# A planner that counts late inputs and holds engines for one chain

## The chip, the cores and the metric

The kernel runs on one core of a Trainium2 chip. What is measured is the device time of one execution in microseconds. The core has five engines with a list of instructions each, worked through in order: TensorE (PE in the profile, its weight loads PEld), VectorE (DVE), ScalarE (ACT), GpSimd (POOL) and SyncE (SP), which here issues the transfers.

## What is computed

Block-sparse attention and then a feed-forward layer with a rational function, in float32, for 4 batches, 8 heads, 768 positions and 64 values a head. A row of 32 positions (a block) sees its neighbours, the first and the last block, and three sampled ones; the first and the last block see all.

```
scores = scale * q @ k.T          # masked by blocks
attn   = softmax(scores)
x      = (attn @ v) as 3072 x 512
h      = x @ w_in                 # 512 x 2048
g      = (a0 + a1 h + a2 h^2 + a3 h^3) / (1 + |b0||h| + |b1| h^2 + 1e-6)
out    = g @ w_out                # 2048 x 512
```

## The kernel before

**Work.** Float32 values are carried as pairs of 16-bit values (a high and a low half), scaled by a power of two that comes from a maximum. So k, q, x and w_in each need the maximum of their magnitudes (ScalarE, L400 in `bound`), a transpose on TensorE that spreads it over the partitions (`most` in `scales`, L351), a few tiny VectorE instructions (L356 to L368), the high half (any of three engines, L150 or L154) and the low half (VectorE, L394 for q and k). The halves of k and q are then transposed on TensorE into a bank of PSUM named sp (L683 for k of batches 1 to 3, L758 for q) and copied out by ScalarE (L150 into kt, L762 into qa). From qa two transfers make a swapped copy qc (L766, L767). From kt a transfer stores k to DRAM (L697), from where the sampled blocks are loaded later (L876 to L883).

The attention works on blocks: scores into sp (L911), masked maxima on VectorE (L921), exponentials (L939), transposes (L980), values (L1037). Four blocks make a group that is weighted by VectorE (L1071), transposed (L1109) and cut into the high half xh (L150) and the low half xl (L1125). Eight blocks are a chunk of 256 positions, 12 chunks in all. The feed-forward layer takes a chunk in 8 units: 24 matmuls of 256 columns into ph (L1179 to L1181), some ten instructions of ScalarE and VectorE for the rational function (L1186 to L1224), and 12 matmuls of 512 columns into acc (L1235 to L1237). The first chunk has no scale of its batch yet: its own maximum is taken from the transposed x (L400 on ph, L1094) and goes through `scales` as scx before any unit can begin. Early idle time of TensorE is filled with matmuls of an identity whose result is not used (L162).

**Order.** All of it is written down first as a list of `Op`s: an engine, a price in ns, the ops it comes after, a priority (`prio`, in units of the feed-forward layer), and the buffers that it takes and uses (`Slot` of a `Ring`; two banks for sp, two buffers for qa, one for hlq and ldq, two for hl). `issue` then simulates the engines and emits instructions in the order of that simulation; each engine runs them in that order on the chip, waiting where an input is late. An op becomes ready on an engine at `at`, the end of what it comes after plus a latency by pair of engines plus 17 ns. Among the ops that have their buffers, the one with the smallest key is next: the time at which it could start, less 21 ns but not before the engine is free, then its priority. An op whose priority lies over 8 units ahead of the work begun is passed over.

```
t = max([now[e], o.at[e]] + [s.ring.free[0][0] for s in o.takes])
key = (max(t - slack, now[e]) + (0 if e == o.engs[0] else other[e]), o.prio, o.n)
```

So the order on TensorE follows the planned times of inputs, those of transfers among them, and nothing corrects it on the chip.

Of the kernel before, what the change touches and what calls it, by code (L numbers as in the profile page):

```python
# [23 lines left out]
def kernel(  # L24
# [70 lines left out]

    VE, SC, PO, TE, SY = "DVE", "Activation", "Pool", "PE", "SP"
    LAT = {(SC, TE): 410, (VE, TE): 240, (PO, TE): 225, (TE, SC): 200, (TE, VE): 200, (TE, SY): 170, (VE, SC): 130, (VE, PO): 130,
           (SC, VE): 155, (SC, PO): 180, (PO, VE): 80, (PO, SC): 100}
# [6 lines left out]
    class Ring:  # L105


        def __init__(self, bufs):
            self.free = [(0.0, b) for b in bufs]
# [7 lines left out]
    class Op:  # L117


        def __init__(self, eng, price, run, after=(), prio=0.0, takes=(), uses=(), unit=None, behind=None):  # L120
            self.alt = eng if isinstance(eng, dict) else None
            self.engs = list(eng) if self.alt else [eng]
            self.eng, self.price, self.run, self.prio, self.unit = self.engs[0], price, run, prio, unit
            self.after, self.behind = [a for a in after if a is not None], behind
            self.takes, self.uses = list(takes), list(takes) + list(uses)
            for s in self.uses:
                s.left += 1
            self.next, self.at, self.work = [], dict.fromkeys(self.engs, 0.0), 1.0
            plan.append(self)

    plan = []
# [32 lines left out]
    def issue(ahead):  # L164
# [29 lines left out]
        while left:  # L194
            best = None
            for e, l in todo.items():
                for o in l:
                    if o.prio > clock + ahead or not all(s.ring.free for s in o.takes):
                        continue
                    t = max([now[e], o.at[e]] + [s.ring.free[0][0] for s in o.takes])  # L200
                    if e == SY:
                        t = max(t, lanes[0])
                    if e == VE and held[0] <= t < held[1] and o.run.__name__ not in READS_PSUM:
                        t += HELD * (held[1] - t)
                    key = (max(t - slack, now[e]) + (0 if e == o.engs[0] else other[e]), o.prio, o.n)
                    if best is None or key < best[0]:
                        best = key, t, o, e
# [57 lines left out]
            for x in o.next:  # L265
                if x.behind is not o:
                    for y in x.engs:
                        lat = MARGIN if isinstance(price, list) else OWN.get(e, 0) if y == e else LAT.get((e, y), 160) + MARGIN
                        x.at[y] = max(x.at[y], end + lat)
                x.wait -= 1  # L270
                if not x.wait:
                    for y in x.engs:
                        todo[y].append(x)
# [68 lines left out]

    def scales(get, name, after, prio, slot=(), finish=None, keep=None):

# [30 lines left out]

        a = Op(TE, 109, most, after, prio, takes=[s_ps])
        a = Op(VE, 260, largest, [a], prio, takes=slot, uses=[s_ps])
# [178 lines left out]
    def prep(b, when, what):  # L556
# [11 lines left out]
        for w in what:  # L568
# [40 lines left out]
            if w == 2:  # L609
                def largest(mx=mx):  # L610
                    nc.vector.tensor_reduce(out=mx[0][:, 6:7], in_=mx[0][:, 0:n], axis=AX.X, op=ALU.max)

                o = Op(VE, 75, largest, los, when(w, 0, n - 1))
                q_scale[b] = scales(lambda mx=mx: mx[0][:, 6:7], "scqb", [o], when(w, 0, n - 1))
                continue

            def largest(mx=mx, w=w):
# [4 lines left out]
                           keep=lambda s, inv, w=w: kv[b].__setitem__(2 + w, inv),  # L622
                           finish=out_scale if w and b < PLAIN else None)
            (k_scale, v_scale)[w][b] = o
# [13 lines left out]
    def rest(b, w, j, d, o_scale, sc, prio, before):  # L638
# [59 lines left out]

        o = Op(TE, 445, transposes, [o], prio, takes=[s_ps], uses=[s_hl])
        sk = s_kall[t] if first else s_kt[b]  # L700
# [12 lines left out]
    def prep_q(b, t, prio, before):  # L713
# [57 lines left out]
        if own:  # L771
            o = Op(SC, 613, most, [o_ld], prio, uses=[s_ld])
            o, sc = scales(lambda: d["mx"][:, 0:1], "scq", [o], prio, sl_sc)
        else:
            o, sc = q_scale[b]
# [5 lines left out]
        else:  # L781
            d["first"], d["oc"] = qt[b, 0], qt[b, 0]["oc"]
        x = Op(TE, 445, transposes, [l], prio, takes=[s_ps, d["slot"]], uses=[s_hl])
        x = Op(SC, 904, evac, [x], prio, uses=[s_ps, d["slot"]])
        d["oq"] = Op(SY, [(650, 131072)] * 2, swap, [x], prio, uses=[d["slot"]])
# [44 lines left out]
    def attention(b, j, prio):  # L830
# [245 lines left out]
        oinv = row(VE, [(70, guard), (81, invert)], [o for o in G["ops"] if o.eng != TE], p, uses=[G["s_sm"]])  # L1076
        G["ops"] = [Op(VE, 600, weigh, [o for o in G["ops"] if o.eng == TE] + [oinv], p, takes=[G["s_xn"]], uses=G["av"] + [G["s_sm"]])]
        if c:
            turned(G, c, e2, p)
            evacuate(G, c, e2, p, kv[b], 4, v_scale[b])  # L1080
            return
# [20 lines left out]
        for G, e2, p, _ in x_wait:  # L1102
            evacuate(G, c, e2, p, x_own, 1, o)

    def turned(G, c, e2, p):
# [302 lines left out]
```

## Time and profile before

| | us |
|---|---|
| median of 3 runs | 883.95 |
| the runs | 875.47, 883.95, 887.24 |
| the profiled execution | 879.92 |
| its span | 878.2 |
| TensorE busy | 827.3 (94%) |
| VectorE busy | 725.5 (83%) |
| ScalarE busy | 675.9 (77%) |

The span runs from the first to the last instruction in the profile, and the profiled execution's own time is 1.7 us longer. In the rows further below, "[1.81 <-DVE hlq L394]" behind an instruction says that its engine was idle for 1.81 us before it, and that the VectorE instruction of line 394 that writes hlq ended this. In the table of stretches PEclk is the granted clock of TensorE as a share of 2.4 GHz.

### The profile page before, as it was taken

What the parts mean: (1) busy time and instruction counts of PE and PEld (TensorE: products, weight loads), DVE (VectorE), ACT (ScalarE), POOL (GpSimd) and SP (SyncE); (2) the same over time, 40 slices, a digit from 0 to 9 for tenths busy, and PEclk for the clock granted to TensorE, in tenths of its full rate; (3) what the DMA queues carried; (4) which work ended last, traced back from release to release, by engine and by line L of the source; (5) the groups of instructions that cost most, each with busy time, mean ns of one, the idle gap of its engine ahead of it and who ended that gap; (6) DMA issues with size and microseconds to landing.
All of it is one profiled execution on the core that took longest, in us unless ns stands there. A gap on an engine that the chain in (4) does not pass through costs nothing.

```text
span 878.2 us, 28042 instructions
## 1 busy us (share of the span) xinstructions
PE 827.3 (94%) x10338; PEld 642.6 (73%) x10338; DVE 725.5 (83%) x1746; ACT 675.9 (77%) x1450; POOL 112.3 (13%) x117
## 2 busy tenths in 40 slices
PE   8989868779899899999999999999999899999997
PEld 4456756657678687778878787778778788778886
DVE  6778998999998787787878686888888688778886
ACT  5789988987787788897777687897767587767563
POOL 1146426164300000100000000100000000000000
PEclk9999988998999999999999999999999999999999
DMA  8697799868656966888556956889545965740000
GB/s 195 154 215 224 209 206 202 217 205 215 140 152 169 282 156 175 216 241 229 140 147 177 250 164 172 216 222 242 147 137 160 235 159 155 179 108 26 1 26 24
DMA packets 240216, 151.22 MB, mean 172 GB/s; under 512 B 16208, under 2 KB 222928, under 8 KB 240080
## 3 DMA queue, kind: packets, MB, share of 16 engines
q1 hardware_dynamic: 240080, 149.43, 65.7%
q8 instruction: 82, 1.34, 0.7%
q14 instruction: 54, 0.44, 0.2%
HBM read 132.07 MB, written 11.01 MB: 163 GB/s over the span
## 4 chain that ended last, share of the span: by engine, by line
PE 62%; DVE 11%; DMA 9%; SPq 7%; ACT 6%; issue 3%; POOL 1%; ACTq 0%; POOLq 0%; DVEq 0%
PE acc L1235 8%; PE ph L1179 8%; PE acc L1236 8%; PE acc L1237 8%; PE ph L1180 7%; PE ph L1181 7%; PE av L1037 5%; PE sp L911 4%; PE pt L980 4%; DMA ldq<-in_q_dram 2%; DMA wl<-in_moe_w_in_dram 2%; SPq L1007 1%; DMA vg<-in_v_dram 1%; DMA ld<-in_v_dram 1%; DVE pr L921 1%
## 5 line engine op out<-in xcount | busy, mean ns | idle before, releaser
L1179 PE MATMUL ph<-xh,wi 128*128 128x256 f16 x768 | 214.1, 279 | 4.7 <-DVE tt L1196 3.6
L1181 PE MATMUL ph<-xh,wi 128*128 128x256 f16 x768 | 212.5, 277 | 2.2 <-POOL wi L514 2.2
L1180 PE MATMUL ph<-xl,wi 128*128 128x256 f16 x768 | 212.6, 277 | 0.1
L1235 PE MATMUL acc<-wo_h,gh 128*128 128x512 f32 x376 | 160.8, 428 | 0.0
L1237 PE MATMUL acc<-wo_h,gl 128*128 128x512 f32 x376 | 149.4, 397 | 3.3 <-DVE gl L1224 3.3
L1236 PE MATMUL acc<-wo_l,gh 128*128 128x512 f32 x376 | 149.4, 397 | 0.0
L1203 DVE SCALAR_TENSOR_TENSOR ab<-sq,absb,ab 128x512 f32<-128x512 f32 x96 | 73.4, 764 | 53.4 <-ACT ab L1200 53.3
L1186 ACT ACTIVATE sq<-ph,fc 128x512 f32<-128x512 f32 x96 | 65.8, 685 | 65.9 <-PE ph L1181 65.5
L1179 PEld LDWEIGHTS <-wi 128*128 128x128 f16 x768 | 76.3, 99 | 34.5 <-issue 17.4
L921 DVE CUSTOM_DVE_ANT_1 pr<-sp,bias 128x256 f32<-128x256 f32 x224 | 84.8, 418 | 10.1 <-PE sp L911 10.0
L1214 DVE SCALAR_TENSOR_TENSOR gh<-tt,par,rr 128x512 fp32r<-128x512 f32 x96 | 75.7, 789 | 17.0 <-PE acc L1236 12.2
L939 ACT ACTIVATE pr<-pr,st,cqb 128x256 f32<-128x256 f32 x112 | 66.1, 594 | 29.6 <-DVE st L950 29.4
L1237 PEld LDWEIGHTS acc<-wo_h,gl 128*128 128x128 f32 x376 | 71.0, 189 | 22.2 <-DVE gl L1224 5.1
L1181 PEld LDWEIGHTS <-wi 128*128 128x128 f16 x768 | 76.4, 99 | 12.7 <-POOL wi L514 2.5
L1235 PEld LDWEIGHTS acc<-wo_h,gh 128*128 128x128 f32 x376 | 71.4, 190 | 17.5 <-issue 1.9
L1037 PE MATMUL av<-vg,pT 128*32 128x64 f32 x3584 | 74.4, 224 | 9.5 <-DMA vg<-in_v_dram 5.6
L1180 PEld LDWEIGHTS <-wi 128*128 128x128 f16 x768 | 76.5, 100 | 9.3 <-issue 0.9
L1037 PEld LDWEIGHTS av<-vg,pT 128*32 128x32 f32 x3584 | 56.6, 111 | 34.4 <-issue 11.9
L1236 PEld LDWEIGHTS acc<-wo_l,gh 128*128 128x128 f32 x376 | 71.4, 190 | 11.4
L980 PE MATMUL pt<-ident,pr 128*128 128x128 f32 x448 | 74.8, 288 | 3.3 <-ACT pr L939 3.0
L980 PEld LDWEIGHTS pt<-ident,pr 128*128 128x128 f32 x448 | 67.6, 204 | 13.0 <-ACT pr L939 5.3
L150 ACT ACTIVATE pT<-pt 128x512 f32<-128x512 f32 x112 | 66.5, 593 | 12.5 <-PE pt L980 11.8
(185 smaller groups left out, 1661.0 us busy)
## 6 DMA issues: line engine op xcount, KB each, us to landing
vg<-in_v_dram SPq DMA_DIRECT2D x312, 64.0 KB, 3.1
vg<-in_v_dram SPq DMA_DIRECT2D x88, 192.0 KB, 3.8
vg<-in_v_dram SPq DMA_DIRECT2D x24, 512.0 KB, 5.4
kall<-ks SPq DMA_DIRECT2D x52, 192.0 KB, 3.3
kall<-ks SPq DMA_DIRECT2D x156, 64.0 KB, 2.3
ld<-in_k_dram SPq DMA_DIRECT2D x36, 256.0 KB, 3.5
wl<-in_moe_w_in_dram SPq DMA_DIRECT2D x32, 256.0 KB, 4.9
wl<-in_moe_w_out_dram SPq DMA_DIRECT2D x16, 512.0 KB, 4.3
```

The costliest lines, as they stand in the source:

```text
L150: nc.scalar.activation(out=out, in_=in_, func=AF.Copy, scale=by)
L921: nc.vector.tensor_tensor_reduce(out=prs[x][:, g].rearrange("p (s r) -> p s r", r=BLK), in0=h["sp"][:, g].rearrange("p (s r) -> p s r", r= ...
L980: nc.tensor.transpose(pp[:, jj * P:(jj + 1) * P], cols, ident)
L1037: nc.tensor.matmul(av[rows, g], pT[:, 2 * g + kt, rows] if plain else pT[:, 2 * g + kt, pa_, rows], vf[:, g * HG + h4, kt * D:(kt + 1) * D ...
L1179: nc.tensor.matmul(o, wh, xh[:, :, cc], start=(cc == 0), stop=False)
L1180: nc.tensor.matmul(o, wh, xl[:, :, cc], start=False, stop=False)
L1181: nc.tensor.matmul(o, wl, xh[:, :, cc], start=False, stop=(cc == NCC - 1))
L1203: nc.vector.scalar_tensor_tensor(out=d["ab"], in0=d["sq"], scalar=absb[:, 1:2], in1=d["ab"], op0=ALU.mult, op1=ALU.add)
L1214: nc.vector.scalar_tensor_tensor(out=d["gh"], in0=d["tt"], scalar=par[:, 0:1], in1=d["rr"], op0=ALU.add, op1=ALU.mult)
L1235: nc.tensor.matmul(acc[:, t], ghs, wo_h[:, f], start=(new and e == 0), stop=False)
L1236: nc.tensor.matmul(acc[:, t], ghs, wo_l[:, f], start=False, stop=False)
L1237: nc.tensor.matmul(acc[:, t], gls, wo_h[:, f], start=False, stop=(last and e == 1))
```

## The change

An `Op` gets a number `late` (0 unless given) that is added to the time at which its inputs count as ready, and a number `rush` (0 unless set) that is taken off in the key: an op that could start in up to 600 ns is then chosen ahead of one that could start now, and the engine is kept for it. `late` is 1500 ns for the spreading transposes of the scales of k, v and q in batches 1 to 3 and for the transposes of k and q in these batches; the scales of w_in and of the first chunk's x keep 0. `rush` is set on the second group of the first chunk (chunk 0): its weighting, transposes, maximum, scale, and the halves of x of both groups. Besides, the buffer qa is taken by the copy out of PSUM and no longer by the q transposes in front of it.

```
+    LATE = 1500.0
...
-            self.after, self.behind = [a for a in after if a is not None], behind
+            self.after, self.behind, self.rush = [a for a in after if a is not None], behind, 0.0
...
-                    key = (max(t - slack, now[e]) + (0 if e == o.engs[0] else other[e]), o.prio, o.n)
+                    key = (max(t - slack - o.rush, now[e]) + (0 if e == o.engs[0] else other[e]), o.prio, o.n)
...
-                        x.at[y] = max(x.at[y], end + lat)
+                        x.at[y] = max(x.at[y], end + lat + x.late)
...
-    def scales(get, name, after, prio, slot=(), finish=None, keep=None):
+    def scales(get, name, after, prio, slot=(), finish=None, keep=None, late=0.0):
...
-        a = Op(TE, 109, most, after, prio, takes=[s_ps])
+        a = Op(TE, 109, most, after, prio, takes=[s_ps], late=late)
...
-                q_scale[b] = scales(lambda mx=mx: mx[0][:, 6:7], "scqb", [o], when(w, 0, n - 1))
+                q_scale[b] = scales(lambda mx=mx: mx[0][:, 6:7], "scqb", [o], when(w, 0, n - 1), late=LATE)
...
-                           finish=out_scale if w and b < PLAIN else None)
+                           late=LATE if b else 0.0, finish=out_scale if w and b < PLAIN else None)
...
-        o = Op(TE, 445, transposes, [o], prio, takes=[s_ps], uses=[s_hl])
+        o = Op(TE, 445, transposes, [o], prio, takes=[s_ps], uses=[s_hl], late=0.0 if first else LATE)
...
-            o, sc = scales(lambda: d["mx"][:, 0:1], "scq", [o], prio, sl_sc)
+            o, sc = scales(lambda: d["mx"][:, 0:1], "scq", [o], prio, sl_sc, late=LATE if b else 0.0)
...
-        x = Op(TE, 445, transposes, [l], prio, takes=[s_ps, d["slot"]], uses=[s_hl])
-        x = Op(SC, 904, evac, [x], prio, uses=[s_ps, d["slot"]])
+        x = Op(TE, 445, transposes, [l], prio, takes=[s_ps], uses=[s_hl], late=LATE if b else 0.0)
+        x = Op(SC, 904, evac, [x], prio, takes=[d["slot"]], uses=[s_ps])
...
+        first = len(plan) - 1
         if c:
...
+        for o in plan[first:]:
+            o.rush = 600.0
```

## Rows read from the trace of the kernel before

**Rows 1.** The page: busy us of each engine, its share of the span and its instructions.

```profile
PE 827.3 (94%) x10338; PEld 642.6 (73%) x10338; DVE 725.5 (83%) x1746; ACT 675.9 (77%) x1450; POOL 112.3 (13%) x117
```

**Rows 2.** The table by stretches: from and to, length, then busy us of PE, PEld, DVE, ACT and POOL with their instructions, the granted clock, the busy share of the transfer engines, GB/s.

```profile
100.00:120.00 20.00, 14.17 (x292) 11.30 (x292) 20.00 (x48) 18.50 (x46) 6.89 (x7) 0.96 0.84 169
...
300.00:350.00 50.00, 50.00 (x652) 40.77 (x652) 40.43 (x108) 43.08 (x97) 0.98 (x1) 1.00 0.65 175
```

**Rows 3.** Waits of TensorE at the lines that the change touches, asked for from 100 to 200 us (the first two) and from 200 us to the end: who waited for whom, us in total, times, longest.

```profile
PE sp L683 <- ACT kt L150: 1.9, 2, 1.4
PE sp L758 <- DVE cq L749: 1.4, 1, 1.4
...
PE sp L758 <- DVE hlq L394: 5.5, 3, 2.2
...
PE sp L351 <- DVE mx L618: 0.8, 1, 0.8
...
PE sp L683 <- DVE hl L394: 0.6, 1, 0.6
PE sp L683 <- DVE st L921: 0.6, 1, 0.6
```

**Rows 4.** Timelines of GpSimd, VectorE and TensorE around the waits at 487 and 687 us: start and length in us, instruction, and in brackets the idle time before it.

```profile
487.59 0.69 POOL L154 TENSOR_SCALAR hlq<-ldq,scqb 128x512 f16<-128x512 f32 x1 [37.46 <-DMA ldq<-in_q_dram]
...
488.31 0.75 DVE L394 SCALAR_TENSOR_TENSOR hlq<-ldq,scqb,hlq 128x512 f16<-128x512 f32 x1 [4.45 <-POOL hlq L154]
...
489.12 0.62 PE L758 MATMUL sp<-ident,hlq 128*128 128x128 f16 x8 [1.81 <-DVE hlq L394]
...
684.57 0.28 PE L1179 MATMUL ph<-xh,wi 128*128 128x256 f16 x1
...
685.79 0.27 PE L1181 MATMUL ph<-xh,wi 128*128 128x256 f16 x1
...
688.86 1.04 PE L758 MATMUL sp<-ident,hlq 128*128 128x128 f16 x8 [2.22 <-DVE hlq L394]
689.69 0.42 PE L1179 MATMUL ph<-xh,wi 128*128 128x256 f16 x1
```

**Rows 5.** The table by stretches again (columns as in rows 2), close around three waits at L758.

```profile
490.00:494.00 4.00, 4.00 (x58) 2.65 (x51) 4.00 (x11) 3.50 (x7) 0.00 (x0) 0.57 1.10 350
686.00:692.00 6.00, 3.78 (x52) 2.99 (x52) 3.94 (x10) 1.06 (x3) 0.69 (x1) 0.72 1.10 246
...
548.00:552.00 4.00, 4.00 (x76) 3.21 (x77) 3.86 (x9) 3.02 (x5) 0.00 (x0) 1.00 0.65 179
```

**Rows 6.** Timelines of TensorE, ScalarE and VectorE on the chain of the first chunk's scale.

```profile
64.45 0.60 PE L1109 MATMUL ph<-ident,xn 128*128 128x128 f32 x4
...
65.17 1.00 ACT L863 COPY kx<-kall 128x256 f16 x3
66.08 0.58 ACT L400 ACTIVATE scrap<-ph 128x512 f16<-128x512 f32 x1
...
67.52 4.48 PE L162 MATMUL acc<-ident 128*128 128x512 f16 x20
71.84 0.27 PE L1179 MATMUL ph<-xh,wi 128*128 128x256 f16 x1
...
68.61 0.15 DVE L1097 COPY xs<-scx 128x1 f32<-128x1 f32 x1
...
68.85 1.30 ACT L762 ACTIVATE qa<-sp 128x1024 f16<-128x1024 f16 x1
70.02 1.24 ACT L150 ACTIVATE xh<-ph,xs 128x512 f16<-128x512 f32 x2
...
70.72 1.41 DVE L1125 SCALAR_TENSOR_TENSOR xl<-ph,xs,xh 128x512 f16<-128x512 f32 x2 [1.43 <-ACT xh L150]
...
79.80 0.23 PE L911 MATMUL sp<-kall,qa 128*32 128x96 f16 x4
```

**Rows 7.** Timelines of VectorE and TensorE for the last two q tiles. Of the last but one: the transposes (712.23) and the first score (736.69). Of the last: the low half (716.68), the last score of the tile two back (728.10), the transposes (736.15).

```profile
712.23 0.34 PE L758 MATMUL sp<-ident,hlq 128*128 128x128 f16 x3
...
716.68 0.74 DVE L394 SCALAR_TENSOR_TENSOR hlq<-ldq,scqb,hlq 128x512 f16<-128x512 f32 x1
...
728.10 0.28 PE L911 MATMUL sp<-kall,qc 128*32 128x256 f16 x4
...
736.15 0.33 PE L758 MATMUL sp<-ident,hlq 128*128 128x128 f16 x3
...
736.69 0.29 PE L911 MATMUL sp<-kall,qa 128*32 128x256 f16 x4
```

**Rows 8.** Timelines of SP and TensorE at the start of batches 2 and 3: the first load of sampled k and the first scores; then from the page the time of such a load from issue to landing (issues, KB each, median us).

```profile
398.38 1.82 SPq L878 DMA_DIRECT2D kall<-ks  x1
...
601.22 1.49 SPq L878 DMA_DIRECT2D kall<-ks  x1
...
413.36 0.29 PE L911 MATMUL sp<-kall,qa 128*32 128x256 f16 x4
...
615.41 0.29 PE L911 MATMUL sp<-kall,qa 128*32 128x256 f16 x4
...
kall<-ks SPq DMA_DIRECT2D x52, 192.0 KB, 3.3
```

More of the change, by code (lines that the diff above doesn't have):

```diff
@@ L117, with __init__ @@
     class Op:
-        def __init__(self, eng, price, run, after=(), prio=0.0, takes=(), uses=(), unit=None, behind=None):
+        def __init__(self, eng, price, run, after=(), prio=0.0, takes=(), uses=(), unit=None, behind=None, late=0.0):
             self.alt = eng if isinstance(eng, dict) else None
@@ L127, in __init__ @@
                 s.left += 1
-            self.next, self.at, self.work = [], dict.fromkeys(self.engs, 0.0), 1.0
+            self.next, self.at, self.work, self.late = [], dict.fromkeys(self.engs, 0.0), 1.0, late
             plan.append(self)
```

## The prediction, made before the change was run

> **What bounds the kernel now.** I read four views in this order. First the page's engine rows [rows 1]: TensorE is busy 827.3 of 878.2 us, VectorE 725.5, ScalarE 675.9. Then the table by stretches [rows 2], since one average hides two regimes. From 100 to 120 us VectorE is the full engine (20.00 of 20 us) and TensorE is not (14.17); from 300 to 350 us TensorE is the full one (50.00 of 50 us) while VectorE lies at 40.43. The reader should see that idle TensorE time counts in full only in the second regime, which I let begin at 200 us. Third, the waits of TensorE before and after 200 us [rows 3], of which I keep the lines that end in an instruction the change touches: L758 (transposes of q), L683 (transposes of k), L351 (the transpose that spreads a scale). Fourth, timelines of the places named below.
>
> In the second regime TensorE waited 5.5 us in three waits at the q transposes, 0.8 us at a scale and 0.6 + 0.6 us at the k transposes, together 7.5 us; shorter waits at these lines are left out. The longest two show how such a wait arises [rows 4]: GpSimd had waited for the q load, VectorE stood 4.45 us behind GpSimd, and TensorE, which runs its list in order, stood 1.81 us at the transposes, although what follows them needs neither. At 688 us it is the same with 2.22 us; 5.5 - 1.8 - 2.2 leaves 1.5 us for the third. The order had been written for a load that came sooner.
>
> **The change, part by part.**
>
> *The late price (1500 ns on inputs of preparing transposes, batches 1 to 3).* No instruction is added or removed. The planner now believes that those inputs come 1.5 us later, so it puts about 1.5 us of other TensorE work in front. A wait can shrink by its own length or by 1.5 us, whichever is less: 3 × 1.5 + 0.8 + 0.6 + 0.6 = 6.5 us. That is one end; the other is nothing, if the work put in front waits just as long. For the three long ones the nearest row says that work is at hand: right behind the transposes of 688.86 the matmuls of a feed-forward unit start at 689.69 with no wait named [rows 4], though VectorE had only just come out of its own stop, so their inputs were older. I take these three in full, 4.5 us, and the short ones as nothing, since under a microsecond another late result of VectorE can stand in.
>
> What is queued behind: a transpose that comes 1.5 us later moves the ScalarE copy and, for q, two transfers on SP by as much. The q tile transposed at 712.23 was read only at 736.69 [rows 7], so more than 20 us cover this; should that cover be gone, the delay goes straight into the scores. The k side has less cover and is the last rival.
>
> *The clock.* The granted clock is 1.00, the upper level of 2.4 GHz, from 300 to 350 us [rows 2]. From 490 to 494 us it is 0.57, from 686 to 692 us 0.72 [rows 5]: parts of these stretches lie at the half level (1.2 GHz), and both follow or hold one of the two long waits. Behind the third, at 548 us, the stretch stays at 1.00. The falls cost 4 × 0.43 = 1.7 us and 6 × 0.28 = 1.7 us of TensorE work. With 1.5 us taken off, 0.3 and 0.7 us of these waits are left, less than the wait before 548 us that brought no fall; I take both back, 3.4 us. The other end is 0, if the falls come elsewhere instead.
>
> *The same price before 200 us.* There 1.4 us (L758, released by cq) and 1.9 us (L683) are waited [rows 3]. VectorE is the full engine in that part, so I count nothing; the other end is a gain of 3.3 us.
>
> *The hold of 600 ns for the first chunk's scale.* Its chain is in [rows 6]. The last transposes of the chunk end at 64.45 + 0.60 = 65.05 us, but ScalarE took three copies for the scores at 65.17 and comes to the maximum (L400 on ph) only at 66.08: 1.0 us. The scale is ready at 68.61 + 0.15 = 68.76; ScalarE took the copy of a q tile at 68.85 and scales x at 70.02: 1.2 us. Together 2.2 us that holding could save, while TensorE issued 20 filling matmuls from 67.52 on that compute nothing, and the first real one came at 71.84. The work that is moved behind is covered: the q tile copied at 68.85 is read at 79.80. Soon after comes VectorE's regime, so what counts is idle time of VectorE: it stood 1.43 us before the low half of x (70.72). I take 1.4 us. The bounds: 2.2 us gained, or, as a price, VectorE kept idle for up to 0.6 us by each of its nine rushed instructions (the weighting, two maxima, three steps of the scale, the copy, two low halves), 5.4 us lost in a regime that has no VectorE time to spare.
>
> *The q slot, taken by the copy and no longer by the transposes.* It lets transposes run before the tile two back is done with. The clearest case is the last tile [rows 7]: its low half was ready at 717.42, the slot free at 728.38, yet it was transposed at 736.15, 7.8 us after that: TensorE had more urgent work. So I cost this at nothing. Were it used, a score bank of two would be held for up to 728.4 - 717.4 - 1.5 = 9.5 us, and the loss lies between nothing and those 9.5 us; nearest is the row that shows the transposes late for another reason, so nothing.
>
> **Sum.** The profiled execution took 879.92 us (span 878.2 and 1.7 around it). 879.9 - 4.5 - 3.4 - 1.4 = 870.6 us. It lies 4.0 us below the median of the three runs (883.95), so beside that median the forecast is 874.6, rounded to **875 us**, 1.0% less. A measurement of this kernel can tell about 2% from no change, here 17.7 us: the three runs alone are 11.8 us apart.
>
> **The rivals.**
>
> *The waits move on, nothing is gained (884 us, the median).* The cause at 487 and 687 us is a late load and a VectorE that stands 4.45 us behind GpSimd [rows 4]; the price is put on TensorE's instructions and brings neither the load nor VectorE's part sooner. TensorE would then pass the transposes and meet the next late result. For it speaks that VectorE is idle in the same microseconds, against it the unit at 689.69. Chance 0.27.
>
> *TensorE is not truly full (884 us too).* Then it makes up a stop of 2 us by itself, and taking the stop away gives nothing. By the rows it is full: twelve matmuls of 256 columns start from 684.57 to 685.79, 11 steps of 0.111 us [rows 4], beside 256 / 2.4 = 107 ns that the columns alone take at the upper clock, and matmuls stand for 50.00 of 50 us in 300 to 350 us [rows 2]. The Trainium skill, "Perfetto Trace Analysis", section "Identifying the Most-Contended Engine", says that the busy share of matmuls is no measure of how close TensorE is to its limit, and that the busy share of weight loads should be read instead. By that rule the stretch is at 40.77 of 50 us, a fifth would be free, and the stops would cost nothing: 884 us. The spacing speaks against it here: 0.08.
>
> *The k preparation gets too long (slower).* Place: the chain of a batch's k, one scale and six sets of transposes, each priced 1.5 us late. If each link also falls behind a half unit, 12 × 0.111 = 1.3 us [rows 4], a link costs 2.8 us and seven of them 19.6 us. Then the last store of a batch, and the loads of its sampled k behind it on SP, come that much later. Those loads start at 398.38 and 601.22 in batches 2 and 3, land some 3.3 us later, and the first scores follow at 413.36 and 615.41 [rows 8]: slacks of 11.7 and 10.9 us. Where the delay exceeds these it decides; the excess is 7.9 + 8.7 = 16.6 us, so 896.5 us, 900.5 beside the median. With the bare 1.5 us per link (10.5 us) it stays below both, so the chance is 0.10.
>
> **How the numbers follow.** Forecast 0.55, moved waits 0.27, TensorE not full 0.08, long k preparation 0.10. The low end takes every gain at its bound on the profiled execution: 879.9 - 6.5 - 3.4 - 3.3 - 2.2 = 864.5. The high end is the first rival with the holds at their price: 884 + 5.4 = 889.4. At either end I add 3.5 us, as the three runs lie 3.3 to 8.5 us from their own median: 861 to 893. Outside stays most of the k rival and a little on either side. Faster by over 2% (below 866.3) needs nearly all bounds at once: 0.11. Slower by over 2% (above 901.6) is half of the k rival: 0.05. Within 2%: 0.84.
>
> **What would show it.** Right: the waits at L758, L683 and L351 after 200 us fall from 7.5 us to below 4, the stretches near 490 and 690 us show a clock of 1.00, and the first real matmul comes near 70 us, not at 71.84. Moved waits: those lines vanish while the waits for gl, pr or pT grow by as much. Long k preparation: the first scores of a batch wait for the k load. Wrong altogether: a new wait of tens of microseconds in the first 200 us, where the whole order is written anew behind the hold.

## The result, and the profile after

The changed kernel takes 893.57 us (median of 6 runs, 893.22 to 894.45), the kernel before 884.43 us beside it (6 runs, 875.47 to 887.24): a ratio of 1.0144, 95% interval 1.0103 to 1.0185, so 1.4% slower. The forecast was 875 us with 861 to 893, so the time lies 0.6 us above the range. The profiled execution took 893.68 us (span 891.9); before it was 879.92 (878.2).

The page's engine row answers to [rows 1]. TensorE is busy 2.7 us longer in a span 13.7 us longer; the work is the same, it only stands differently.

```profile
PE 830.0 (93%) x10333; PEld 646.5 (72%) x10333; DVE 727.2 (82%) x1748; ACT 673.3 (75%) x1447; POOL 113.2 (13%) x118
```

Where the time went is seen first in the start of the 96 units of the feed-forward layer (the first matmul into ph of each). Unit 0 starts 1.8 us earlier than before. Up to unit 9 the distance jumps (unit 7 starts 13.2 us later, unit 9 1.8 us earlier, at 176.18 against 178.01); unit 10 starts 12.0 us later (205.71 against 193.69), unit 20 15.2 us, and from unit 73 on the distance stays at 14.07 us. So most of the loss is there by 206 us, in the part of the run where I had counted nothing. The table by stretches (columns as in rows 2), first before, then after:

```profile
100.00:150.00 50.00, 38.31 (x602) 30.24 (x603) 45.69 (x120) 44.39 (x106) 18.95 (x18) 0.86 0.92 191
150.00:180.00 30.00, 25.56 (x327) 20.23 (x325) 30.00 (x53) 28.77 (x62) 6.44 (x7) 1.00 0.86 224
180.00:206.00 26.00, 19.88 (x273) 14.75 (x271) 25.61 (x68) 21.49 (x49) 18.52 (x17) 0.87 0.68 192
```

```profile
100.00:150.00 50.00, 42.10 (x691) 32.26 (x689) 46.97 (x118) 46.02 (x115) 18.51 (x18) 0.84 0.91 199
150.00:180.00 30.00, 23.23 (x339) 17.88 (x340) 29.45 (x66) 25.18 (x56) 7.76 (x8) 0.86 0.86 206
180.00:206.00 26.00, 15.38 (x158) 11.46 (x156) 18.62 (x46) 18.92 (x43) 17.47 (x16) 0.74 0.69 220
...
300.00:350.00 50.00, 50.00 (x669) 40.44 (x667) 43.72 (x123) 41.02 (x94) 1.38 (x2) 1.00 0.67 184
```

VectorE, which had 0.4 us of idle time from 150 to 206 us, now stands idle for 7.4 of the last 26 us, and TensorE's clock is 0.74 there. The regime behind it looks as before.

What stopped them between 180 and 206 us, by the longest wait of TensorE from 170 to 215 us and by timelines of TensorE, ScalarE, VectorE and SP:

```profile
PE sp L1113 <- ACT kt L151: 7.6, 1, 7.6
```

```profile
179.71 1.10 PE L684 MATMUL sp<-ident,hl 128*128 128x128 f16 x16
...
183.10 0.65 PE L1038 MATMUL av<-vg,pT 128*32 128x64 f32 x32 [1.17 <-ACT pT L151]
191.39 1.12 PE L1113 MATMUL sp<-ident,xn 128*128 128x128 f32 x4 [7.64 <-ACT kt L151]
192.30 0.42 PE L352 MATMUL sp<-ident,mxq 128*128 128x128 f32 x1
...
185.52 0.79 ACT L1194 ACTIVATE tt<-ph,par,fc 128x512 f32<-128x512 f32 x1
...
188.92 0.63 ACT L151 ACTIVATE wi<-dw 128x512 f16<-128x512 f32 x1 [1.49 <-POOL dw L155]
189.46 2.47 ACT L151 ACTIVATE kt<-sp 128x512 f16<-128x512 f16 x4
...
186.34 0.69 DVE L1197 TENSOR_TENSOR tt<-tt,sq 128x512 f32<-128x512 f32 x1 [3.07 <-ACT tt L1194]
...
192.76 0.29 DVE L357 TENSOR_REDUCE scq<-sp 128x1 f32<-128x128 f32 x1 [2.61 <-PE sp L352]
...
179.68 0.40 SPq L698 DMA_DIRECT2D ks<-kt  x1
```

TensorE transposed the last two k tiles of batch 1 together at 179.71 (sixteen transposes) into the two banks of sp. Their copies go into kt, which is still being stored (issued at 179.68, landed at 185.40), and ScalarE's list reaches them only at 189.46, behind copies of w_in, for one of which it stands idle 1.49 us itself. Until then no bank is free for the x transposes (L1113), and behind these in TensorE's list stands the transpose that spreads the scale of a q tile (L352), for which VectorE waits at 192.76. A second group of stops lies at 157 to 163 us, where TensorE waits 2.90 us for VectorE's masked maxima and 1.58 us for its tt. Its waits from 150 to 170 us:

```profile
PE sp L684 <- DVE st L922: 2.9, 1, 2.9
PE ph L1183 <- DVE tt L1200: 1.9, 2, 1.6
```

To weigh all stops alike I add up **TensorE's lost time** from the timeline: its idle time in front of instructions (the 4.4 to 4.9 us behind its last one are left out), the time of the filling matmuls (L163 after, L162 before), and for real matmuls under a lower clock the part that the clock takes. Before it is 88.9 us up to 206 us and 18.0 us after, together 106.9; in the changed kernel 101.3 and 22.3, together 123.6. What is left of the span is 771.3 and 768.3 us. Of the 12.4 us that are added up to 206 us, 5.7 lie between 150 and 180 us (4.5 before, 10.2 after) and 5.7 between 180 and 206 us (8.7 before, 14.4 after). So the 7.6 us stop stands for no more than half of the loss.

### The profile page after: what moved, and what is told of

Same layout as the page of the kernel before. It is cut to its first block, busy times and chain, and to the rows that moved or that the text cites. A ratio compares the mean times of both kernels' runs of the same rounds, so it can differ in the third digit from the quotient of the medians.

```text
span 891.9 us, 28046 instructions
## 1 busy us (share of the span) xinstructions
PE 830.0 (93%) x10333; PEld 646.5 (72%) x10333; DVE 727.2 (82%) x1748; ACT 673.3 (75%) x1447; POOL 113.2 (13%) x118
## 4 chain that ended last, share of the span: by engine, by line
PE 63%; DVE 11%; DMA 8%; ACT 7%; SPq 6%; issue 3%; POOL 1%; ACTq 0%; POOLq 0%; DVEq 0%
PE acc L1239 8%; PE ph L1183 8%; PE acc L1240 8%; PE acc L1241 8%; PE ph L1184 7%; PE ph L1185 7%; PE av L1038 5%; PE sp L912 4%; PE pt L981 4%; ACT pr L940 2%; DMA ld<-in_v_dram 2%; DMA wl<-in_moe_w_in_dram 2%; SPq L1008 1%; DMA ld<-in_k_dram 1%; DMA ldq<-in_q_dram 1%
## 5 line engine op out<-in xcount | busy, mean ns | idle before, releaser
L1241 PE MATMUL acc<-wo_h,gl 128*128 128x512 f32 x376 | 151.4, 403 | 2.2 <-DVE gl L1228 2.2
L1218 DVE SCALAR_TENSOR_TENSOR gh<-tt,par,rr 128x512 fp32r<-128x512 f32 x96 | 72.5, 755 | 21.3 <-PE acc L1240 19.8
L1185 PEld LDWEIGHTS <-wi 128*128 128x128 f16 x768 | 75.9, 99 | 10.2 <-issue 0.5
L1240 PEld LDWEIGHTS acc<-wo_l,gh 128*128 128x128 f32 x376 | 72.6, 193 | 13.2 <-POOL wo_l L468 1.2
L981 PE MATMUL pt<-ident,pr 128*128 128x128 f32 x448 | 77.0, 293 | 3.1 <-ACT pr L940 1.6
L940 ACT ACTIVATE pr<-pr,st,cq 128x256 f32<-128x256 f32 x112 | 66.0, 592 | 12.5 <-DVE st L951 12.4
```

The costliest lines, as they stand in the source:

```text
L940: nc.scalar.activation(out=prs[x][:, g], in_=prs[x][:, g], func=AF.Exp, scale=Q["first"]["c"], bias=st[:, 6 + g:7 + g], accum_out=total if ...
L981: nc.tensor.transpose(pp[:, jj * P:(jj + 1) * P], cols, ident)
L1185: nc.tensor.matmul(o, wl, xh[:, :, cc], start=False, stop=(cc == NCC - 1))
L1218: nc.vector.scalar_tensor_tensor(out=d["gh"], in0=d["tt"], scalar=par[:, 0:1], in1=d["rr"], op0=ALU.add, op1=ALU.mult)
L1240: nc.tensor.matmul(acc[:, t], ghs, wo_l[:, f], start=False, stop=False)
L1241: nc.tensor.matmul(acc[:, t], gls, wo_h[:, f], start=False, stop=(last and e == 1))
```

## The experiments

The table has all kernels: the median time and its ratio to the kernel before, run beside it on the same chip, then from the profiled execution VectorE's idle time from 100 to 206 us (summed over the timeline) and TensorE's lost time up to and after 206 us.

| kernel | edit | median us | ratio, 95% interval | VectorE idle | lost to 206 / after |
|---|---|---|---|---|---|
| before | | 884.43 | | 4.7 | 88.9 / 18.0 |
| after | whole change | 893.57 | 1.0144 [1.0103, 1.0185] | 10.9 | 101.3 / 22.3 |
| e3_hold_only | hold alone | 892.86 | 1.0157 [1.0101, 1.0212] | 11.4 | 99.5 / 21.1 |
| e4_late_only | late price alone | 881.76 | 1.0017 [0.9989, 1.0044] | 5.9 | 88.4 / 20.2 |
| e1_k_plain | change, k transposes not late | 892.33 | 1.0148 [1.0092, 1.0203] | 13.1 | 102.0 / 19.8 |
| e2_kt_first | change, kt taken before transposing | 895.08 | 1.0166 [1.0108, 1.0224] | 11.9 | 104.4 / 24.0 |
| f1_k45_after_x | change, two k tiles behind x | 899.02 | 1.0205 [1.0167, 1.0243] | 9.4 | 96.6 / 32.5 |
| f4_one_bank | change, last k tile behind copies | 888.87 | 1.0096 [1.0066, 1.0126] | 8.8 | 97.9 / 24.1 |
| e9_neutral | before, margin 16 ns, not 17 | 879.92 | 0.9997 [0.9958, 1.0036] | 7.2 | 86.4 / 15.1 |
| e6_hold_100 | hold alone, 100 ns | 880.69 | 0.9993 [0.9956, 1.0031] | 4.7 | 87.4 / 19.1 |
| e7_hold_200 | 200 ns | 880.22 | 0.9975 [0.9936, 1.0015] | 7.0 | 86.6 / 20.7 |
| e8_hold_300 | 300 ns | 882.43 | 1.0017 [0.9981, 1.0054] | 2.9 | 85.6 / 22.8 |
| e10_hold_450 | 450 ns | 882.64 | 1.0029 [1.0000, 1.0059] | 7.5 | 90.6 / 19.5 |
| e11_hold_500 | 500 ns | 879.75 | 0.9988 [0.9954, 1.0022] | 6.2 | 91.5 / 17.4 |
| e12_hold_550 | 550 ns | 886.04 | 1.0052 [1.0020, 1.0083] | 6.0 | 90.5 / 18.7 |
| e13_hold_700 | 700 ns | 897.55 | 1.0189 [1.0134, 1.0244] | 12.2 | 97.8 / 25.2 |
| e14_hold_900 | 900 ns | 888.04 | 1.0050 [1.0009, 1.0090] | 8.6 | 91.7 / 24.0 |
| e15_change_hold_200 | whole change, hold 200 ns | 887.92 | 1.0101 [1.0064, 1.0139] | 7.1 | 88.1 / 28.3 |
| e16_change_hold_500 | whole change, hold 500 ns | 882.04 | 1.0035 [1.0009, 1.0060] | 7.2 | 89.7 / 16.9 |

What the span holds beside the lost time lies between 766.9 and 772.9 us in all of them. The numbers of the last two columns come from one execution each: after, e3_hold_only and e1_k_plain have the same lists of instructions up to 202.7 us at least, and yet differ by 2.2 us in VectorE's idle time and by 2.5 us in lost time up to 206 us. The slot of qa has no run of its own: moved alone it gives the same list of instructions on every engine as before.

**Which part.** The hold alone (late price 0, slot as before), and the late price alone:

```
-    LATE = 1500.0
+    LATE = 0.0
...
-        x = Op(TE, 445, transposes, [l], prio, takes=[s_ps], uses=[s_hl], late=LATE if b else 0.0)
-        x = Op(SC, 904, evac, [x], prio, takes=[d["slot"]], uses=[s_ps])
+        x = Op(TE, 445, transposes, [l], prio, takes=[s_ps, d["slot"]], uses=[s_hl], late=LATE if b else 0.0)
+        x = Op(SC, 904, evac, [x], prio, uses=[s_ps, d["slot"]])
```

> The kernel before with the 600 ns hold alone; no late price, no moved slot. Theory (the hold writes the first 200 us anew and brings the k units 4 and 5 of batch 1 together, with the group's transposes right behind them): 890 to 895 us, a wait of 5 to 9 us at the transposes of x for a copy into kt near 190 us. Rival (the late price causes it): 880 to 886 us, no such wait.

```
-            o.rush = 600.0
+            o.rush = 0.0
```

(here too with the slot as before)

> The kernel before with the 1500 ns late price alone; no hold, no moved slot. Theory: 879 to 887 us, no long wait for kt before 206 us, and after 200 us the waits at the preparing transposes fall from 7.5 to under 4 us while those for pT rise to 8 us or more, so that nothing is gained. Rival (the late price causes the loss): 890 to 896 us. If the prediction's second-regime terms hold after all: 872 to 878 us.

The hold alone is as slow as the whole change, the late price alone is not slower than before. Up to 202.7 us the hold alone has the instructions of the whole change in the same order on every engine, so what is lost by then is the hold's. It shows the same stop, to 10 ns; its longest wait of TensorE from 170 to 215 us, and its stretch from 180 to 206 us, with VectorE idle as in the change:

```profile
PE sp L1113 <- ACT kt L151: 7.6, 1, 7.6
```

```profile
180.00:206.00 26.00, 14.33 (x156) 10.58 (x154) 18.64 (x48) 18.91 (x43) 17.10 (x15) 0.80 0.68 220
```

The late price alone does not even shorten its own waits, and those for pT do not grow to the 8 us that I expected; TensorE's waits from 206 to 860 us:

```profile
PE sp L759 <- DVE hlq L395: 5.9, 2, 3.5
PE av L1038 <- ACT pT L151: 3.8, 3, 2.2
PE sp L759 <- DVE xl L1129: 1.0, 1, 1.0
```

For hlq, 5.9 us at the q transposes stand against 5.5 in [rows 3]: two waits where there were three, the longest now 3.5 us where it was 2.2.

**Is the late k transpose or the early bank at fault?** First, within the change, k transposes without the late price; second, kt taken before the banks of sp are:

```
-        o = Op(TE, 445, transposes, [o], prio, takes=[s_ps], uses=[s_hl], late=0.0 if first else LATE)
+        o = Op(TE, 445, transposes, [o], prio, takes=[s_ps], uses=[s_hl])
```

> The changed kernel without the late price on the k transposes alone; it is the same program up to the k of batch 2. Theory and rival alike 891 to 895 us up to there; if the late k transposes of batches 2 and 3 cost or gain something, the difference is read after 350 us: the theory says within 2 us either way.

```
-        ... takes=[s_ps], uses=[s_hl], late=0.0 if first else LATE)
+        ... takes=[s_ps] + ([s_kt[b]] if g == 0 and not first else []), uses=[s_hl], late=0.0 if first else LATE)
...
-        a = ... takes=[sk] if g == 0 else [], uses=[s_ps] + ([] if g == 0 else [sk]))
+        a = ... takes=[sk] if g == 0 and first else [], uses=[s_ps] + ([] if g == 0 and first else [sk]))
```

> The changed kernel, but the k transposes of batches 1 to 3 may only be placed once the buffer kt is free, so that no score bank is held while a store of kt is under way. Theory (two k units hold both score banks from 180 to 191 us, behind a store and a ScalarE list that comes to the copy late): 882 to 887 us, no wait of TensorE over 3 us for a copy into kt. Rival (the loss lies in the new order of the first 200 us as a whole, the 7.6 us wait is only where it shows): 890 to 896 us, the delay comes up elsewhere before 206 us.

Neither helps. The first keeps the wait of 7.6 us, so the late price of k is no part of it. In the second the wait is gone (five of 1.6 to 2.7 us take its place between 183 and 204 us), yet VectorE is idle for nearly as long (6.95 of the 26 us, in the change 7.4): the tiles wait for kt in SBUF and no longer in the banks, and the k chain ends later (its last store is issued at 198.28, in the change at 191.95).

**Mending the one stop.** The two k tiles put behind the x transposes; then only the last k tile put behind the copies of the one before it, so that a single bank can be held:

```
+ ... [o] + ([x_group[2, 0]["turned"]] if b == 1 and j >= 4 else [])
```

> The changed kernel, with the transposes of the last two of the six k tiles of batch 1 made to follow the x transposes of the third block of output (order the same as in the changed kernel up to about 180 us). Theory: the loss sits in the stop at 180 to 199 us, where these two k tiles hold both of TensorE's small banks for 11 us each while the x transposes, which the next two half units wait for in the end, find no bank. Then the 7.6 us wait is gone, VectorE idles under 3 us between 180 and 206 us instead of 7.4, unit 10 starts before 199 us, and the time is 880 to 886 us. Rival: with the hold the order of the first 200 us is dear as a whole, and the stop only shows where it comes out; then TensorE waits elsewhere, VectorE's idle time at 180 to 206 us stays over 5 us, and the time is 889 us or more.

```
+ ... [o] + ([k_evac[b, t][1]] if b == 1 and j == 5 else [])
```

> The changed kernel, with the transposes of the last k tile of batch 1 made to follow the copies of the one before it, so that only one of the two small banks can be held by a copy that waits for the store. Theory that both banks are needed for the stop: the x transposes go through the other bank, the wait of 7.6 us falls under 3 us, and the time is 880 to 887 us. Rival, that ScalarE's late copies into the block (its list reaches them at 189 us) and the decoding behind them are what costs: the k chain only gets longer, as with the block taken first (895 us), and the time is 889 to 896 us.

Both remove the wait, and the theory that the loss sits in this stop falls with the first, at 899 us. The second, at 888.87 us, lies between the ranges of its theory and its rival. The longest waits of TensorE from 170 to 215 us in the first, and its stretch from 180 to 206 us:

```profile
PE pt L981 <- ACT pr L940: 2.7, 1, 2.7
PE sp L759 <- ACT kt L151: 2.3, 1, 2.3
```

```profile
180.00:206.00 26.00, 18.89 (x221) 14.44 (x221) 20.42 (x52) 20.00 (x43) 15.08 (x15) 0.80 0.90 267
```

The same two views of the kernel with the last k tile alone put back:

```profile
PE sp L912 <- DVE st L922: 4.5, 2, 3.0
PE av L1038 <- ACT pT L151: 1.8, 1, 1.8
```

```profile
180.00:206.00 26.00, 18.57 (x204) 13.08 (x205) 21.55 (x49) 19.98 (x42) 14.70 (x15) 0.74 0.67 211
```

TensorE's lost time up to 206 us falls by 4.7 and 3.4 us of the 12.4 that the change had added. VectorE is still idle for 5.6 and 4.4 of the 26 us, and all kernels with 600 ns lose 9.2 to 10.4 us between 150 and 170 us (before: 2.8, by the same sum), which these edits do not touch. Behind 206 us the first then loses 10 us more than the change did. So the 7.6 us wait is at most a part of the loss, and how large a part is not shown: the second kernel's ratio of 1.0096 lies below the change's 1.0144, but their intervals overlap.

**How long a hold?** Any new order might be slower than a tuned one, so a neutral edit stands beside three short holds (the first diff is on top of the hold alone, the second of the kernel before; the other holds differ in the number alone).

```
-            o.rush = 600.0
+            o.rush = 100.0
```

```
-    ... MARGIN = 17.0
+    ... MARGIN = 16.0
```

> The kernel before with the hold alone, at 100 ns in place of 600. Three theories. Holding costs by its length: a sixth of the 12 us, so 882 to 885 us. The place of batch 1's k transposes in TensorE's list decides (here at rows 2170 to 2513, before 2362 to 2613, changed 2465 to 2694): 876 to 883 us. Any new order of the first 200 us is another draw, no matter how small the cause: anything from 878 to 898 us, with the loss in TensorE's idle time, filling and slow clock before 206 us.

> The same with 200 ns. By length: 884 to 887 us. By place (k transposes of batch 1 at rows 2490 to 2895, later than in the changed kernel): 893 to 900 us. Another draw: anything from 878 to 898 us.

> The same with 300 ns. By length: 886 to 889 us. By place (rows 2237 to 2561, earlier than before): 877 to 884 us. Another draw: anything from 878 to 898 us.

> The kernel before with no hold and no late price; only the planner's margin on every latency is 16 ns in place of 17, which means nothing on the chip and writes the order anew (k transposes of batch 1 at rows 2314 to 2564). By length: 879 to 883 us, as nothing is held. By place: 878 to 884 us. Another draw: it may lose as much as the hold, 885 to 897 us.

All four are at the time before, with VectorE idle for 2.9 to 7.2 us. So none of these four new orders costs anything that can be told. The theory of length falls at 200 and 300 ns, where it had 884 us and more, and the theory of place at 200 ns, where it had 893 us and more. Then the longer ones:

> The hold alone at 450 ns, without the late price and with the slot where it was. Theory (the loss is made by what the planner can put together once the chain is held, and not by the held time itself): either no loss or nearly the whole, depending on whether batch 1's last k tiles come together in front of the x transposes: 879 to 884 us or 889 us and more, and VectorE's idle time at 180 to 206 us says which (about 1 us or about 7 us). Rival (the loss grows with the hold's length from 300 ns on): halfway, 885 to 889 us, with VectorE idle 3 to 5 us there.

> The hold alone at 500 ns. Theory (only the one order that 600 ns gives has the loss, since its stops at 157 to 168 and 183 to 199 us come from what stands next to what in that order): 878 to 885 us, VectorE idle under 3 us between 180 and 206 us. Rival (a hold of 500 ns or more is too long, whatever order comes of it): 888 to 895 us, VectorE idle over 5 us there.

> The hold alone at 550 ns. Theory (one order alone): 878 to 885 us and VectorE idle under 3 us between 180 and 206 us. Rival (a long hold is dear by itself): 888 to 895 us, and VectorE idle over 5 us there.

> The hold alone at 700 ns. Theory (one order alone): 878 to 885 us and VectorE idle under 3 us between 180 and 206 us. Rival (a long hold is dear by itself): 888 to 896 us, and VectorE idle over 5 us there.

> The hold alone at 900 ns. Theory (one order alone): 878 to 886 us and VectorE idle under 3 us between 180 and 206 us. Rival (a long hold is dear by itself, the longer the dearer): 890 to 900 us, and VectorE idle over 5 us there.

At 450 and 500 ns the theories came true. At 550, 700 and 900 ns neither side's range is met, and VectorE's idle time from 180 to 206 us, the sign that I had named, fails: it is 1.6, 0.0 and 0.25 us, although 700 ns is the slowest hold. No hold alone up to 500 ns is told from before (450 ns lies at the edge of its interval); 550 and 900 ns cost 0.5%, 600 and 700 ns 1.6 and 1.9%, so each of the four beyond 500 ns costs, but not the more the longer. At 700 ns the stops lie elsewhere; its longest waits of TensorE from 150 to 215 us, and its stretch from 150 to 180 us:

```profile
PE acc L1241 <- DVE gl L1228: 5.2, 1, 5.2
PE ph L1183 <- DVE tt L1200: 5.2, 2, 4.0
PE sp L1113 <- ACT kt L151: 3.9, 1, 3.9
```

```profile
150.00:180.00 30.00, 20.30 (x230) 15.16 (x231) 25.92 (x54) 18.65 (x39) 7.60 (x8) 0.83 0.55 119
```

Here ScalarE works 18.65 of 30 us and VectorE 25.92, where before they had 28.77 and 30.00. With the stretch widened to 100 to 206 us, after the fact, the table shows what these kernels share: those with VectorE idle for over 9 us take 892 us or more, the two between 8.6 and 8.8 us take 888 and 889, and those under 7.6 take 880 to 886, with one exception, which is the next run. These steps are finer than the 2.2 us by which executions of the same lists differ. TensorE's lost time up to 206 us parts the kernels with a wider gap: the seven with 96.6 us or more take 888.87 us or more, the others (91.7 or less) 888 or less.

**The whole change with a shorter hold** (200 and 500 ns in place of 600).

> The whole change, but with 200 ns as the hold instead of 600. Theory (the loss belongs to long holds, by VectorE's idle time between 100 and 206 us, and the late price makes no difference in the end): VectorE idle under 7.6 us between 100 and 206 us, and 876 to 885 us. Rival (the late price and any hold together make the loss): 888 to 895 us.

> The whole change, but with 500 ns as the hold. Theory (up to 500 ns costs nothing): VectorE idle under 7.6 us between 100 and 206 us, and 876 to 886 us. Rival (500 ns is at the edge, and with the late price the order has the stops again): VectorE idle over 8.5 us there, and 887 to 896 us.

The second came as expected, though it is still 0.35% slower than before, just clear of the noise. The first has the VectorE time expected and TensorE's 88.1 us of lost time up to 206 us, no more than before, and is still 1.0% slower: it loses 28.3 us behind 206 us. Its longest waits of TensorE from 206 to 860 us:

```profile
PE sp L759 <- DVE hlq L395: 6.7, 3, 3.3
PE av L1038 <- ACT pT L151: 5.7, 4, 3.5
PE pt L981 <- ACT pT L151: 2.7, 1, 2.7
PE sp L912 <- ACT kt L151: 2.4, 1, 2.4
PE sp L912 <- DMA xkg<-ks: 2.0, 1, 2.0
```

The q transposes wait longer here than before the change (6.7 against 5.5 us), and four other groups of waits of 2 us and more join them. The hold of 200 ns without the late price loses only 20.7 us there, and its ratio (0.9975) lies clear of this one (1.0101). So a short hold does not make the whole change free, and the theory of VectorE's idle time covers the first 206 us only; behind them every order has its own late inputs.

## Why the prediction was wrong, step by step

**The hold: -1.4 us, bounds -2.2 and +5.4. This step failed.** Its first half came true. Timelines of VectorE, ScalarE and TensorE after, against [rows 6]:

```profile
65.77 0.15 DVE L1099 COPY xs<-scx 128x1 f32<-128x1 f32 x1
...
66.05 0.63 ACT L401 ACTIVATE scrap<-ld 128x512 f16<-128x512 f32 x1 [1.77 <-DMA ld<-in_v_dram]
...
66.68 1.92 ACT L864 COPY kx<-kall 128x256 f16 x6
68.51 1.25 ACT L151 ACTIVATE xh<-ph,xs 128x512 f16<-128x512 f32 x2
...
70.03 0.28 PE L1183 MATMUL ph<-xh,wi 128*128 128x256 f16 x1 [0.85 <-DVE xl L1129]
```

The scale is ready at 65.92 us where it was 68.76, 2.8 us sooner. ScalarE first stood 1.77 us for a v load, took six copies for the scores, and scaled x 1.5 us sooner than before; the first real matmul came 1.8 us sooner. (The two waits on ScalarE that I set out to save come to 1.03 + 1.26 = 2.3 us, not 2.2.) The price was looked for in the wrong place: I bounded it by the held time of nine VectorE instructions, but VectorE's idle time from 60 to 100 us did not grow (4.2 us after, 4.7 before). The price came 80 to 140 us later, in the order that the planner wrote behind the hold, and at 12.4 us (10.6 in the execution of the hold alone) it is about twice my bound. I had named this case ("wrong altogether", a new wait of tens of microseconds in the first 200 us), without a chance or a place in the range; it came as many waits, the longest of 7.6 us. That the time lies only 0.6 us above the range is no merit: its high end holds 5.4 us for VectorE kept idle by the hold and 3.5 us for the spread of the runs, and neither is what happened.

**"VectorE is the full engine there, so I count nothing." This premise failed too.** [rows 2] show VectorE full from 100 to 120 us, and in that kernel it idles for only 0.4 us from 150 to 206 us. But the queue that feeds it is an order, and a full engine stays full only while its inputs come: 7.4 us of its time were lost where TensorE and ScalarE stood. Nor was TensorE's time free there. In all 19 kernels the span is its lost time, the early part included, plus 766.9 to 772.9 us: most of what TensorE does not do by 206 us it does behind it, where it is full.

**The late price: -4.5 us. This term failed too.** The sign of it that I named came: the waits at L759, L684 and L352 behind 200 us fell from 7.5 to 2.4 us, below 4. The gain did not, as in the rival "the waits move on": waits for pT grew from 2.6 to 12.9 us, more than the others fell. TensorE's waits after, from 200 us on:

```profile
PE av L1038 <- ACT pT L151: 12.9, 6, 4.2
...
PE sp L759 <- DVE hlq L395: 1.3, 1, 1.3
PE sp L684 <- ACT kt L151: 1.1, 1, 1.1
```

The longest two are at 276.64 and 500.17 us. Timelines of ScalarE, VectorE and TensorE at the second show late q loads as in [rows 4], now with ScalarE in the list in front:

```profile
497.30 0.63 ACT L401 ACTIVATE scrap<-ld 128x512 f16<-128x512 f32 x1 [4.47 <-DMA ld<-in_q_dram]
...
497.56 0.75 DVE L395 SCALAR_TENSOR_TENSOR hlq<-ldq,scqb,hlq 128x512 f16<-128x512 f32 x1 [6.62 <-POOL hlq L155]
...
500.17 1.08 PE L1038 MATMUL av<-vg,pT 128*32 128x64 f32 x32 [4.24 <-ACT pT L151]
```

But the late price is not what moved them. The hold alone, without any late price, has no wait left at the q transposes behind 206 us, and it stops for pT behind the same q tile. Its largest group of waits of TensorE from 200 us on, and timelines of VectorE and TensorE:

```profile
PE av L1038 <- ACT pT L151: 9.0, 5, 4.7
```

```profile
495.83 0.75 DVE L395 SCALAR_TENSOR_TENSOR hlq<-ldq,scqb,hlq 128x512 f16<-128x512 f32 x1 [7.19 <-POOL hlq L155]
...
499.05 1.08 PE L1038 MATMUL av<-vg,pT 128*32 128x64 f32 x32 [4.75 <-ACT pT L151]
```

So the new order behind the hold decides which instruction meets the late load. Four pairs of kernels differ by the late price (in three of them with the slot): with it the waits of the q transposes for hlq went from 5.5 to 5.9 us without a hold, from 4.7 to 6.7 with 200 ns, from 5.6 to 2.2 with 500 ns and from none to 1.3 with 600 ns. The ratio to before went from 1 to 1.0017, from 0.9975 to 1.0101, from 0.9988 to 1.0035 and from 1.0157 to 1.0144. None of the four shows a gain that can be told; the second shows a loss.

**The clock: -3.4 us.** This term failed as well. At the two times that I named the clock is now 1.00, but this kernel is some 14 us behind there. Around the wait that ends at 500.17 us, with the same q tile, it falls again; stretches after, against [rows 5]:

```profile
490.00:494.00 4.00, 4.00 (x27) 3.31 (x28) 0.94 (x2) 2.52 (x4) 0.00 (x0) 1.00 1.21 239
498.00:504.00 6.00, 3.83 (x47) 3.00 (x48) 6.00 (x14) 4.62 (x13) 0.00 (x0) 0.72 1.13 273
686.00:692.00 6.00, 6.00 (x68) 4.89 (x65) 5.33 (x10) 4.82 (x10) 0.00 (x0) 1.00 0.52 137
```

Only the second fall is gone (1.00 also from 700 to 706 us), and two others came near 278 and 377 us, behind waits for pT (0.72 from 276 to 282 us, 0.79 from 374 to 382 us). Behind 206 us the lower clock took 4.7 us of real matmuls, 1.5 more than before (3.2).

**The signs.** All that I had named under "Right" came: the waits below 4 us, the clock of 1.00 at the two places, the first real matmul at 70.03 us. They look only at the places that I had priced, and the time was lost elsewhere.

**The q slot: nothing.** Right: the same list of instructions.

**The rivals.** "TensorE is not truly full", so that stops cost nothing, is refuted: TensorE's lost time and the span move together, 12.4 and 4.3 us more lost (before and behind 206 us), 3.0 us less rest, 13.7 us more span. The rest is not quite constant: through the 19 kernels a straight line gives 0.85 us of span for 1 us of lost time, so a small part is made up. The rule that spoke for this rival (the Trainium skill, "Perfetto Trace Analysis", section "Identifying the Most-Contended Engine") reads TensorE's headroom from two numbers, the arithmetic done as a share of the peak and the busy share of weight loads; I used the second alone. By it, 40.44 of 50 us from 300 to 350 us would leave a fifth free, while the spacing of 0.111 us in the prediction leaves 4% over the 107 ns of the columns. The long k preparation did not happen: no wait of TensorE behind 200 us ends with a load of sampled k, and without the late price on k the time is the same.

**What stays open.** Shown is that the hold of 600 ns is the cause in this change: alone it has the whole loss, by the same lists up to 202.7 us, the late price alone has none, and with 500 ns 0.35% is left. Not shown is that the length of a hold is what costs. With 200 ns the whole change still loses 1.0%, in another place, and why the orders of 600 and 700 ns run into such stops and those of 500 and 900 ns less or not at all was not settled. A neutral edit beside the hold of 600 ns, which would tell a long hold from this one order, was not run. The stops of 600 ns at 150 to 170 us were seen, not mended; by the same sum 550 and 900 ns lose 8.9 us there and cost only 0.5%. That VectorE's idle time is the way the loss comes about is a reading that fits 18 of 19 kernels, with borders drawn after 17 of them were known; of the two that tested it one fits.

## What to carry to other kernels

When a planner's rule is changed, the held or delayed instruction can be the small part, as it was here; price the order that comes behind it, by the spread of a few neighbouring settings, before trusting a sum over the waits that the rule aims at. A wait that vanishes at the place aimed at need not have been ended by the part that aimed at it: run each part alone. And an engine that is not the full one in a stretch still pays there, if it is the one whose total sets the end.

## What the hardware showed unexpectedly

The granted clock fell differently in the same order of work. The whole change and the hold alone have the same lists of instructions up to 202.7 us, but from 100 to 150 us the clock was 0.84 in one (above) and 0.96 in the other:

```profile
100.00:150.00 50.00, 37.98 (x689) 29.39 (x687) 46.56 (x116) 45.47 (x114) 17.87 (x18) 0.96 0.89 198
```

Up to 206 us the lower clock took 15.0 us of real matmuls in the first and 7.4 in the second, but the idle time was 39.9 against 45.6 us, and the sums with the filling matmuls differ by 1.8 us only (101.3 and 99.5). The change without the late price on k, a third execution of these lists, fits in: 16.4 us by the clock, 38.2 us idle, 102.0 in all. So where TensorE waited for others anyway, most of what the lower clock took came out of its waits.
